# GeGLU on one core: raw rows of the first down projection fetched in front of stores, and the first pass's x transposed wholly on TensorE

## The chip, the cores and the metric

The kernel runs on one core of one Trainium2 chip. The metric is the device time of one execution in microseconds. A profile is one execution with every instruction recorded; its span is 1.7 to 2.2 us shorter than the device time of the same execution, for every kernel here.

Names used below: PE is TensorE, DVE is VectorE, ACT is ScalarE, POOL is GpSimd, SP is the engine that issues nearly all DMAs ("SPq" is its queue of instructions). `Lnnn` is a line of the kernel; many operations go through a helper and share its line. The granted clock is PE's clock as a share of full speed; PE is called cold while it is below 1. The DMA share is the mean busy share of the core's 16 DMA engines; transfers are counted in the window in which they start, so a short window can show a little over 1.

## The reference, cut to what matters

```python
B, S, Dm, Df = 1, 2048, 1024, 3584        # all bf16
def reference(x, w_gate, w_up, w_down):
    g = jnp.einsum("bsd,df->bsf", x, w_gate)
    u = jnp.einsum("bsd,df->bsf", x, w_up)
    h = _gelu(g) * u
    return jnp.einsum("bsf,fd->bsd", h, w_down)
```

## The kernel before

Rows of x are worked on in two passes of 1024 rows, each pass as two tiles of 512 rows (`xT[0]`, `xT[1]`, held transposed). A pass has 14 units, each of which makes 256 columns of `g` and `u` and from them a piece of `h`, and then a down projection. Both halves use a scheme with seven instead of eight block products, whose factors are sums of blocks: the `t` and `s` tiles in the units, the `m`/`made`, `td` and `q` tiles in the down projection. The sums of `w_down` are made once, in the first pass, stored to DRAM (`td`), and loaded from there by both passes. The two weight sums made last, of blocks 12 and 13, live in large buffers of the pool "w", which has three; the down projection's 1 MB loads of `td` use the same three buffers.

The down projection advances in steps. In steps 0 to 27 a step is four matmuls of 512 columns (0.86 us) that need raw rows of `w_down` (`rl`, fetched two blocks at a time by `fetch12`); from step 28 on it needs the sums (`q12`).

```python
    AT12 = [2, 2, 5, 5, 8, 8, 16, 18, 20, 22, 27, 29, 31, 33]   # step of each load12
    ...
    def store_made(j):
        nc.sync.dma_start(out=td[:, j], in_=made[j][:, :3].bitcast(f32))

    def load12(j):
        if j in BIG12:                                # BIG12 = (0, 2, 4): 1 MB each
            big = wpool.tile([P, 2, 2, N], f32, name="w")
            nc.sync.dma_start(out=big, in_=td[:, j : j + 2, :2])
    ...
    def fetch12(n):
        kh, j = n // 7, 2 * (n % 7)
        rl = slot([P, 2, N], bf16, "raw")
        nc.sync.dma_start(out=rl, in_=wdn[:, kh, j : j + 2, :N])
        raw[1, n] = rl
    ...
    for n in range(NJ):
        at(max(-1, 2 * n - 6), fetch12, n)            # needed from step 2 * n
    for j in range(NJ):
        at(AT12[j], load12, j)
    ...
            def prepare():                            # in every unit, first pass
                ...
                if js:                                # last unit: js = [11, 12, 13]
                    store_made(js[0])                 # waits for DVE's last sum of block 11
                for j in js[1:]:
                    keep_whole(j)                     # blocks 12, 13: sums on POOL
    ...
        def more(step):                               # runs after the fetches of its step
            if step in (-1, 1):
                store_made(NJ - 2 + (step > 0))       # blocks 12 and 13
            if step >= 16 and step % 2 == 0 and step // 2 - 8 < len(moves):
                c, ko = moves[step // 2 - 8]
                transposing(xT, c, ko, (2 * (ip + 1) + c) * N)    # next pass's x
```

The start: the first tile of x is loaded as rows (`xn`) and transposed on PE in pieces of 128x128 (`turn`), the second is transposed by eight DMAs. The weights of unit 1 come through ACT's queue.

```python
    xn0 = load_x(0)
    wf = wpool.tile([P, 2, NKB, 2 * P], bf16, name="w")
    for k0, k1 in ((0, 2), (2, 5), (5, NKB)):
        load_wf(nc.sync, k0, k1)
    for ko in range(NKB):
        transposing(xT, 1, ko, N)                     # dma_start_transpose
    ...
        for i in range(NS):
            turn(xT, xn0, 0, i, on_act if i == 1 else on_dve)
        w = load_w(1, nc.scalar, pinned=True)
        s = sums_s(w, dve)
        plain(bank[0:4], 0, range(0, 2), parts=2)     # unit 0, tile 0
        plain(bank[0:4], 0, range(2, NKB))
        ...
        plain(bank[4:8], 1, range(NKB))               # unit 0, tile 1
```

Of the kernel before, what the change touches and what calls it, by code (L numbers as in the profile page):

```python
# [10 lines left out]
def kernel(  # L11
# [23 lines left out]
    nc = tc.nc  # L35
    ENG = mybir.EngineType
    ORDER = {ENG.SP, ENG.DVE, ENG.Pool, ENG.PE}
    P = nc.NUM_PARTITIONS
# [12 lines left out]
    NKB = Dm // P  # L51
# [8 lines left out]
    SLOTS = 52  # L60
    LAG = 3
    BIG12 = (0, 2, 4)
    AT12 = [2, 2, 5, 5, 8, 8, 16, 18, 20, 22, 27, 29, 31, 33]
    AT12S = [2 * j + (j > 8) for j in range(NJ)]
    AT73 = [30 + 2 * j if j < 8 else 46 + j - 8 for j in range(NJ)]

# [9 lines left out]
    def new_x():  # L76
        return [xpool.tile([P, NKB, N], bf16, name=f"xT{c}") for c in range(2)]
# [36 lines left out]



    def load_w(u, queue=nc.sync, pinned=False):
        f0 = u * 2 * P
        w = wpool.tile([P, 2, NKB, 2 * P], bf16, name="w")
        for i, src in enumerate((w_gate, w_up)):  # L120
            got = queue.dma_start(
                out=w[:, i],
                in_=src[:, f0 : f0 + 2 * P].rearrange("(ko ki) f -> ki ko f", ki=P),
            )
            if queue is not nc.sync and not pinned:
                tc.keep_in_program_order(got)
        return w

# [7 lines left out]
    def sums_t(xT):  # L136
        K = range(KH)
        lo, hi = [[xT[c][:, k] for k in K] for c in range(2)], [
            [xT[c][:, KH + k] for k in K] for c in range(2)
        ]  # L140
        return Sums(
            how={
                "t1": lambda q: [new(dve, lo[1][k], lo[0][k], SUB, "t1") for k in K],
                "t2": lambda q: [new(dve, hi[1][k], q["t1"][k], SUB, "t2") for k in K],
                "t3": lambda q: [new(dve, hi[1][k], lo[1][k], SUB, "t3") for k in K],
                "t4": lambda q: [new(dve, hi[0][k], q["t2"][k], SUB, "t4") for k in K],
                "tb": lambda q: [cast(hi[1][k], "tb") for k in K],
            }
        )

    def sums_s(w, eng):
        GU = range(2)
        sh = [P, KH, P]
        a11, a21 = [[w[:, i, :KH, h : h + P] for i in GU] for h in (0, P)]
        a12, a22 = [[w[:, i, KH:, h : h + P] for i in GU] for h in (0, P)]
        return Sums(
            how={
                "s1": lambda q: [new(eng, a21[i], a22[i], ADD, "s1", sh) for i in GU],
                "s2": lambda q: [new(eng, q["s1"][i], a11[i], SUB, "s2", sh) for i in GU],
                "s3": lambda q: [new(eng, a11[i], a21[i], SUB, "s3", sh) for i in GU],  # L160
                "s4": lambda q: [new(eng, a12[i], q["s2"][i], SUB, "s4", sh) for i in GU],
                "sa": lambda q: [cast(a22[i], "sa", sh) for i in GU],
            }
        )
# [171 lines left out]
    def at(step, what, j):  # L336
        agenda.setdefault(int(step), []).append((what, j))

    for n in range(NJ):
        at(max(-1, 2 * n - 6), fetch12, n)  # L340
    for j in range(NJ):
        at(AT12[j], load12, j)
        at(AT12S[j], make12, j)
# [88 lines left out]
    def load_x(c):  # L432
        t = []
        for i in range(NS):
            xn = slot([P, Dm], bf16, "xn")
            r0 = c * N + i * P
            nc.sync.dma_start(out=xn, in_=x2[r0 : r0 + P, :])  # L437
            t.append(xn)
        return t
# [4 lines left out]
            nc.tensor.transpose(tp[:, ko, :], xn[i][:, ko * P : (ko + 1) * P], ident)  # L444
        copy(out=xT[c][:, :, i * P : (i + 1) * P], in_=tp)

    def transposing(xT, c, ko, r0):
        nc.sync.dma_start_transpose(  # L448
            out=xT[c][:, ko, :], in_=x2[r0 : r0 + N, ko * P : (ko + 1) * P]
        )  # L450

    def load_wf(queue, k0, k1):
        for i, src in enumerate((w_gate, w_up)):
            got = queue.dma_start(
                out=wf[:, i, k0:k1],
                in_=src[k0 * P : k1 * P, 0 : 2 * P].rearrange(
                    "(ko ki) f -> ki ko f", ki=P
                ),
            )
            if queue is not nc.sync:  # L460
                tc.keep_in_program_order(got)

    xT = new_x()
    xn0 = load_x(0)
    wf = wpool.tile([P, 2, NKB, 2 * P], bf16, name="w")
    for k0, k1 in ((0, 2), (2, 5), (5, NKB)):
        load_wf(nc.sync, k0, k1)
    for ko in range(NKB):
        transposing(xT, 1, ko, N)

    def plain(ps, c, kos, parts=1):
        n = N // parts
        for k in range(kos.start, kos.stop, 2):
            for part in range(parts):
                cols = slice(part * n, (part + 1) * n)
                for p, (j, i) in zip(ps, [(j, i) for j in range(2) for i in range(2)]):
                    for ko in (k, k + 1):
                        matmul(
                            p[:, cols],
                            wf[:, i, ko, j * P : (j + 1) * P],  # L480
                            xT[c][:, ko, cols],
                            ko == 0 and part == 0,
                            ko == NKB - 1,
                        )

    def finish(ps, c):
        for j in range(2):
            times(j, c, gelu(ps[2 * j]), ps[2 * j + 1])

    on_dve, on_act = nc.vector.tensor_copy, nc.scalar.copy  # L490
    t = sums_t(xT)
    with tc.manual_schedule(engines={ENG.Activation}):
        for _ in range(NWARM):
            nc.tensor.matmul(bank[3], lhsT=warm[:, :P], rhs=warm, start=True, stop=True)
        for i in range(NS):
            turn(xT, xn0, 0, i, on_act if i == 1 else on_dve)
        w = load_w(1, nc.scalar, pinned=True)
        s = sums_s(w, dve)
        plain(bank[0:4], 0, range(0, 2), parts=2)
        plain(bank[0:4], 0, range(2, NKB))  # L500
        t.make("t1")
        finish(bank[0:4], 0)
        s.make("s1", "s2")
        t.make("t2", "t3", "tb")
        s.make("s3", "sa")
        plain(bank[4:8], 1, range(NKB))
        finish(bank[4:8], 1)
# [8 lines left out]
    for ip in range(NPASS):  # L516
        for u in range(1 if ip == 0 else 0, NU):
            js = making(u) if ip == 0 else []

            def prepare():  # L520
                nonlocal ahead
                nxt["w"], nxt["s"] = ahead, None
                if u + 1 < NU:
                    nxt["s"] = make_s(ahead, pool)
                if u + 2 < NU:
                    ahead = load_w(u + 2)
                if js:
                    store_made(js[0])
                for j in js[1:]:
                    keep_whole(j)  # L530
                if ip == 0:
                    fetch_wd(making(u + 1))

            def keep(part, ps):
                if js:
                    keep_part(js[0], part, ps)

            def aside(part):
                nonlocal ahead
                if ahead is None:  # L540
                    ahead = load_w(2, nc.scalar)
                if part == 0 and "s4" not in s:
                    s.make("s4")
                    t.make("t4")

            def ahead_of_p4():
                if u + 1 < NU:
                    nxt["p1"] = first_product(even if u % 2 else odd, xT, nxt["w"])

            e = odd if u % 2 else even  # L550
            p1 = nxt.pop("p1", None) or first_product(e, xT, w)
            unit(u, (e, cc, dd), xT, w, s, t, p1, prepare, aside, keep, ahead_of_p4, ip == 0 and u == 1)
            if u + 1 < NU:
                w, s = nxt["w"], nxt["s"]

        last = ip == NPASS - 1
        got, nxt = {}, {}

        def more(step):

            nonlocal ahead
            if last:
                return
            if step in (-1, 1):
                store_made(NJ - 2 + (step > 0))
            if step == 0:
                xT[:] = new_x()
            if step >= 16 and step % 2 == 0 and step // 2 - 8 < len(moves):
                c, ko = moves[step // 2 - 8]
                transposing(xT, c, ko, (2 * (ip + 1) + c) * N)  # L570
            if step == 50:
                got["w"], ahead = load_w(0), load_w(1)
            if step == 58:
                got["s"] = make_s(got["w"], dve)
            if step == 62:
                got["t"] = make_t(xT)

        down(ip, even + cc, dd + odd, last, more)
        even, odd, cc, dd = odd, even, dd, cc
        if not last:  # L580
            w, t, s = got["w"], got["t"], got["s"]
# [29 lines left out]
```

## Time and profile before

| | before |
|---|---|
| time, median of the 3 runs at hand | 549.08 us (548.2 to 550.6) |
| span of the profile | 546.8 us |
| PE busy | 536.2 us, 98% |
| PE waits for raw rows of w_down, first pass | 4.6 us in 4 waits |
| PE waits for x at the start | 0.9 us (xT), 0.5 us (xn) |

PE is busy nearly all the time. These lines of the page are its busy time and the chain of work that ended last:

```profile
PE 536.2 (98%) x2405; PEld 378.7 (69%) x2405; DVE 341.3 (62%) x526; ACT 258.4 (47%) x463; POOL 236.2 (43%) x212
...
PE 92%; DMA 5%; SPq 2%; DVE 0%; issue 0%; ACT 0%; DVEq 0%; ACTq 0%
```

So only the gaps of PE can be won. The view of waits, for PE, has them all (total us, times, longest):

```profile
PE bank L111 <- DMA raw<-in_w_down_dram: 4.6, 4, 1.4
PE bank L494 <- DVE warm L428: 1.2, 1, 1.2
PE bank L111 <- DMA xT<-in_x_dram: 0.9, 2, 0.6
PE bank L444 <- DMA xn<-in_x_dram: 0.5, 1, 0.5
```

The view counts a gap from the modelled end of a matmul. Measured between starts, the four gaps for raw rows are 1.48, 1.52, 1.60 and 0.63 us, 5.2 us in sum. They lie at the head of the first down projection. The windows view of that stretch gives, for each window, its length, the busy time of PE, PEld, DVE, ACT and POOL, the granted clock, the DMA share and GB/s:

```profile
172.00:182.00 10.00, 10.00 (x47) 6.97 (x45) 6.33 (x11) 6.49 (x12) 5.95 (x6) 1.00 0.48 170
182.00:187.00 5.00, 4.42 (x20) 3.44 (x19) 4.09 (x7) 1.75 (x3) 1.04 (x1) 1.00 0.88 269
187.00:197.00 10.00, 8.79 (x40) 3.91 (x40) 9.76 (x16) 0.00 (x0) 0.00 (x0) 1.00 1.03 393
197.00:207.00 10.00, 7.22 (x32) 3.11 (x32) 8.94 (x14) 2.05 (x4) 0.00 (x0) 1.00 1.06 380
```

DMA is half idle before 182 and full after it. The timeline of SP's queue shows why (start, us, what it issued), and so does the first line of its waits from 180 to 216:

```profile
181.89 0.33 SPq L280 DMA_DIRECT2D td<-m  x1
182.31 2.62 SPq L329 DMA_DIRECT2D raw<-in_w_down_dram  x3
185.03 0.45 SPq L280 DMA_DIRECT2D td<-w  x1
185.53 0.42 SPq L329 DMA_DIRECT2D raw<-in_w_down_dram  x1
186.05 1.22 SPq L280 DMA_DIRECT2D td<-w  x1
187.36 1.55 SPq L329 DMA_DIRECT2D raw<-in_w_down_dram  x1
188.96 1.29 SPq L290 DMA_DIRECT2D w<-td  x1
190.30 1.26 SPq L329 DMA_DIRECT2D raw<-in_w_down_dram  x1
191.66 0.59 SPq L290 DMA_DIRECT2D w<-td  x1
```

```profile
SPq L280 <- DVE m L90: 8.6, 1, 8.6
```

SP issued nothing from 173.2 to 181.89, when DVE's sum for the store `td<-m` was made, and all raw fetches stand behind that store; from 180 to 182 the DMA share was 0.00. After it, every raw fetch stands behind a store of 768 KB or a load of 1 MB.

### The profile page before, as it was taken

Reading aid. Unit: us, or ns where it says so; the run is one execution under the profiler, and the core shown is the slowest. Engines: PE = TensorE matmul, PEld = TensorE weight load, DVE = VectorE, ACT = ScalarE, POOL = GpSimd, SP = SyncE. Lnnn points to the kernel's source line nnn. Section 1 sums busy time; section 2 is a strip of 40 time slices with the busy share of each in tenths; the row PEclk is TensorE's granted clock in tenths of the full one; section 3 lists DMA queues with packets and bytes.
Section 4 is the critical chain, followed back from the end, with each engine's and each line's share of the span. In section 5 each row is a group of like instructions: output and inputs, shape, how many; then the busy total and the mean of one; then the engine's idle time right before and its main releaser. Section 6 shows DMA issues by size and latency. Waiting matters only on the chain.

```text
span 546.8 us, 7414 instructions
## 1 busy us (share of the span) xinstructions
PE 536.2 (98%) x2405; PEld 378.7 (69%) x2405; DVE 341.3 (62%) x526; ACT 258.4 (47%) x463; POOL 236.2 (43%) x212
## 2 busy tenths in 40 slices
PE   8999999999999979999999999999999999999997
PEld 5477777667767635888877766776777775478885
DVE  3886766766666893585955555455555449766730
ACT  2466666566656410155445555555555551114431
POOL 0069966677774300000087777777777600000000
PEclk9999999999999999999999999999999999999999
DMA  8776666667645699999745222222222059373751
GB/s 210 168 199 174 173 180 203 197 179 208 199 146 173 229 383 289 308 197 276 263 134 135 78 79 77 78 77 79 77 78 77 0 199 381 133 230 97 226 187 49
DMA packets 108133, 93.28 MB, mean 171 GB/s; under 512 B 17216, under 2 KB 92992, under 8 KB 108096
## 3 DMA queue, kind: packets, MB, share of 16 engines
q1 hardware_dynamic: 103936, 90.72, 56.3%
q10 hardware_dynamic: 4160, 2.10, 1.5%
q8 instruction: 19, 0.31, 0.2%
q14 instruction: 18, 0.15, 0.1%
HBM read 74.45 MB, written 15.20 MB: 164 GB/s over the span
## 4 chain that ended last, share of the span: by engine, by line
PE 92%; DMA 5%; SPq 2%; DVE 0%; issue 0%; ACT 0%; DVEq 0%; ACTq 0%
PE bank L111 92%; DMA raw<-in_w_down_dram 3%; SPq L448 2%; DMA xT<-in_x_dram 1%; DMA xn<-in_x_dram 1%; DVE m L90 0%; SPq L437 0%; ACT bank L269 0%; ACT st L408 0%; SPq L280 0%; ACT u L107 0%; DVEq L90 0%; SPq L329 0%; ACTq L107 0%
## 5 line engine op out<-in xcount | busy, mean ns | idle before, releaser
L93 POOL TENSOR_TENSOR s<-w 128x512 fp32r<-128x512 bf16 x100 | 117.0, 1190 | 191.6 <-DVE t L90 92.8
L111 PE MATMUL bank<-t,s 128*128 128x512 f32 x648 | 157.0, 398 | 0.0
L111 PEld LDWEIGHTS bank<-t,s 128*128 128x128 f32 x648 | 121.8, 188 | 27.7
L111 PE MATMUL bank<-xT,w 128*128 128x512 bf16 (+1 forms) x504 | 116.5, 377 | 0.9 <-DMA xT<-in_x_dram 0.9
L107 ACT COPY p<-bank 128x512 f32<-128x512 f32 x124 | 70.4, 591 | 96.7 <-PE bank L111 96.7
L90 DVE TENSOR_TENSOR hT<-g,bank 128x512 bf16<-128x512 f32 x112 | 76.6, 687 | 54.7 <-ACT g L178 48.9
L111 PEld LDWEIGHTS <-w 128*128 128x128 bf16 x504 | 45.1, 98 | 60.3 <-issue 14.9
L90 DVE TENSOR_TENSOR sum<-bank,p 128x512 f32<-128x512 f32 x54 | 37.4, 692 | 53.2 <-PE bank L111 47.9
L178 ACT ACTIVATE g<-sum 128x512 f32<-128x512 f32 x81 | 51.5, 635 | 32.9 <-DVE sum L90 32.0
L111 PE MATMUL bank<-q 128*128 128x512 f32 x240 | 58.9, 389 | 0.0
L111 PE MATMUL bank<-t,sa 128*128 128x512 f32 x216 | 58.6, 413 | 0.0
L93 POOL TENSOR_TENSOR s<-w,s 128x512 fp32r<-128x512 bf16 x50 | 57.8, 1177 | 0.0
L93 POOL TENSOR_TENSOR s<-s,w 128x512 fp32r<-128x512 f32 x50 | 57.1, 1165 | 0.0
L111 PE MATMUL bank<-raw,hT 128*128 128x512 bf16 x224 | 49.2, 379 | 4.6 <-DMA raw<-in_w_down_dram 4.6
L111 PE MATMUL bank<-tb,s 128*128 128x512 f32 x216 | 53.3, 389 | 0.0
L111 PEld LDWEIGHTS bank<-q 128*128 128x128 f32 x240 | 45.1, 188 | 9.3
L111 PEld LDWEIGHTS bank<-t,sa 128*128 128x128 f32 x216 | 40.7, 188 | 10.6
L111 PEld LDWEIGHTS bank<-tb,s 128*128 128x128 f32 x216 | 40.6, 188 | 8.4
L102 ACT CAST tb<-raw 128x512 fp32r<-128x512 bf16 x28 | 17.2, 627 | 60.5 <-DMA raw<-in_w_down_dram 24.5
L107 ACT COPY u<-bank 128x512 f32<-128x512 f32 x62 | 35.9, 590 | 20.9 <-PE bank L111 19.2
L111 PEld LDWEIGHTS <-hT 128*128 128x128 bf16 x224 | 21.8, 98 | 31.6 <-issue 6.0
L90 DVE TENSOR_TENSOR bank<-bank,p 128x512 f32<-128x512 f32 x54 | 37.8, 700 | 8.2 <-PE bank L111 5.0
(44 smaller groups left out, 459.1 us busy)
## 6 DMA issues: line engine op xcount, KB each, us to landing
raw<-in_w_down_dram SPq DMA_DIRECT2D x80, 256.0 KB, 4.9
q<-td SPq DMA_DIRECT2D x60, 256.0 KB, 4.8
w<-in_w_gate_dram SPq DMA_DIRECT2D x25, 512.0 KB, 5.6
w<-in_w_up_dram SPq DMA_DIRECT2D x25, 512.0 KB, 6.5
td<-m SPq DMA_DIRECT2D x12, 768.0 KB, 4.6
w<-td SPq DMA_DIRECT2D x6, 1024.0 KB, 8.8
out_dram<-st SPq DMA_DIRECT2D x32, 128.0 KB, 1.7
td<-w SPq DMA_DIRECT2D x2, 768.0 KB, 6.7
```

The lines of the kernel that those rows point to most:

```text
L90: nc.vector.tensor_tensor(out=out, in0=a, in1=b, op=op)
L93: nc.gpsimd.tensor_tensor(out=out, in0=a, in1=b, op=op)
L102: nc.scalar.copy(out=t, in_=src)
L107: nc.scalar.copy(out=t, in_=ps)
L111: nc.tensor.matmul(ps, lhsT=lhs, rhs=rhs, start=start, stop=stop, skip_group_check=True)
L178: nc.scalar.activation(g, src, ACT.Gelu_apprx_tanh)
L448: nc.sync.dma_start_transpose(out=xT[c][:, ko, :], in_=x2[r0 : r0 + N, ko * P : (ko + 1) * P])
```

## The change: its intent, and the diff

The raw rows needed first are to be fetched before the stores, while DMA is idle, and everything not needed soon is to come later. At the start, DMA transposes are to be avoided: each takes 1.26 us of SP's time to issue, and PE waited for them. Cut to its core (the removal of helpers that are no longer needed is left out):

```diff
-    AT12 = [2, 2, 5, 5, 8, 8, 16, 18, 20, 22, 27, 29, 31, 33]
+    AT12 = [6, 6, 10, 10, 14, 14, 16, 18, 20, 22, 27, 29, 31, 33]
...
-        at(max(-1, 2 * n - 6), fetch12, n)
+        at(max(-1, 2 * n - 8), fetch12, n)
...
-    for ko in range(NKB):
-        transposing(xT, 1, ko, N)
+    xn1 = load_x(1)
+    w = load_w(1)                       # on SP instead of ACT's queue
...
-        plain(bank[0:4], 0, range(2, NKB))
+        plain(bank[0:4], 0, range(2, 4))
+        for i in range(2):
+            turn(xT, xn1, 1, i, on_act if i % 2 else on_dve)
+        plain(bank[0:4], 0, range(4, 6))
+        for i in range(2, NS):
+            turn(xT, xn1, 1, i, on_act if i % 2 else on_dve)
+        plain(bank[0:4], 0, range(6, NKB))
         (the sums t1, s1, t2, s2 are reordered a little around it)
...
-                if js:
+                if len(js) == 1:
                     store_made(js[0])
...
-            if step in (-1, 1):
-                store_made(NJ - 2 + (step > 0))
+            if step in (-1, 0, 2):
+                store_made({-1: NJ - 3, 0: NJ - 2, 2: NJ - 1}[step])
...
-            if step >= 16 and step % 2 == 0 and step // 2 - 8 < len(moves):
-                c, ko = moves[step // 2 - 8]
+            if step >= 24 and step % 2 == 0 and step // 2 - 12 < len(moves):
+                c, ko = moves[step // 2 - 12]
```

More of the change, by code (lines that the diff above doesn't have):

```diff
@@ L113, in matmul, with load_w @@
         )
-    def load_w(u, queue=nc.sync, pinned=False):
+    def load_w(u, queue=nc.sync):
         f0 = u * 2 * P
@@ L124, in load_w @@
             )
-            if queue is not nc.sync and not pinned:
+            if queue is not nc.sync:
                 tc.keep_in_program_order(got)
@@ L445, in turn @@
         copy(out=xT[c][:, :, i * P : (i + 1) * P], in_=tp)
-    def transposing(xT, c, ko, r0):
-        nc.sync.dma_start_transpose(
-            out=xT[c][:, ko, :], in_=x2[r0 : r0 + N, ko * P : (ko + 1) * P]
-        )
-    def load_wf(queue, k0, k1):
+    xT = new_x()
+    xn0 = load_x(0)
+    wf = wpool.tile([P, 2, NKB, 2 * P], bf16, name="w")
+    for k0, k1 in ((0, 2), (2, 5), (5, NKB)):
         for i, src in enumerate((w_gate, w_up)):
-            got = queue.dma_start(
+            nc.sync.dma_start(
                 out=wf[:, i, k0:k1],
@@ L459, in load_wf @@
             )
-            if queue is not nc.sync:
-                tc.keep_in_program_order(got)
-    xT = new_x()
-    xn0 = load_x(0)
-    wf = wpool.tile([P, 2, NKB, 2 * P], bf16, name="w")
-    for k0, k1 in ((0, 2), (2, 5), (5, NKB)):
-        load_wf(nc.sync, k0, k1)
-    for ko in range(NKB):
-        transposing(xT, 1, ko, N)
+    xn1 = load_x(1)
+    w = load_w(1)
     def plain(ps, c, kos, parts=1):
@@ L490 @@
     on_dve, on_act = nc.vector.tensor_copy, nc.scalar.copy
-    t = sums_t(xT)
+    s, t = sums_s(w, dve), sums_t(xT)
     with tc.manual_schedule(engines={ENG.Activation}):
@@ L496 @@
             turn(xT, xn0, 0, i, on_act if i == 1 else on_dve)
-        w = load_w(1, nc.scalar, pinned=True)
-        s = sums_s(w, dve)
         plain(bank[0:4], 0, range(0, 2), parts=2)
-        plain(bank[0:4], 0, range(2, NKB))
+        plain(bank[0:4], 0, range(2, 4))
[5 more added lines that the diff above has]
+        plain(bank[0:4], 0, range(6, NKB))
         t.make("t1")
+        s.make("s1")
         finish(bank[0:4], 0)
-        s.make("s1", "s2")
-        t.make("t2", "t3", "tb")
+        t.make("t2")
+        s.make("s2")
+        t.make("t3", "tb")
         s.make("s3", "sa")
@@ L563, in more @@
                 return
-            if step in (-1, 1):
-                store_made(NJ - 2 + (step > 0))
+            if step in (-1, 0, 2):
+                store_made({-1: NJ - 3, 0: NJ - 2, 2: NJ - 1}[step])
             if step == 0:
                 xT[:] = new_x()
-            if step >= 16 and step % 2 == 0 and step // 2 - 8 < len(moves):
-                c, ko = moves[step // 2 - 8]
-                transposing(xT, c, ko, (2 * (ip + 1) + c) * N)
+            if step >= 24 and step % 2 == 0 and step // 2 - 12 < len(moves):
+                c, ko = moves[step // 2 - 12]
+                r0 = (2 * (ip + 1) + c) * N
+                nc.sync.dma_start_transpose(
+                    out=xT[c][:, ko, :], in_=x2[r0 : r0 + N, ko * P : (ko + 1) * P]
+                )
             if step == 50:
```

## The prediction

> **What bounds it now.** TensorE: in the page's busy table PE has 98% of a 546.8 us span; the chain of waits is "PE bank" for 92%. Matmuls of 512 columns start 0.214 us apart nearly everywhere, so only PE's gaps can be won. Those that a DMA causes lie in two places (timeline; my gaps are start-to-start distances less the normal one, so a little over its "idle"):
>
> - Start: 0.50 us for xn (at 5.9), 0.50 and 0.74 us for the DMA-transposed xT (18.3 and 21.0).
> - Head of the first down projection: 1.48, 1.52, 1.60 and 0.63 us for raw rows of w_down (187.7, 197.9, 201.2, 205.3), 5.2 us in sum; the waits view says 4.6 us.
>
> The second pass, which stores nothing there, starts the same stage at 455.5 without a gap.
>
> **Why.** In the first pass the first three raw fetches stand in the queue behind a store that waits for DVE's last sum (181.9); the first lands 5.4 us later. DMA idles nearly from 175 to 182. From 182 to 216 it is full (windows view: share 0.9 to 1.12, 288 to 393 GB/s): three stores of 0.77 MB, three loads of 1 MB, raw rows, q loads and six transposes want the same 33 us. The Trainium skill ("DMA: Bandwidth & Descriptors", "Issuing engines are not separate DMA queues") says that all queues run on the same 16 engines and interleave; the saturation agrees, so order and bytes decide, not who issues.
>
> **Down head after.** Four fetches (1 MB, 3 us of DMA at 350 GB/s) go ahead of the stores into the idle time after 173; later ones come two steps (1.7 us) earlier; the 1 MB loads move from steps 2, 5, 8 to 6, 10, 14; six transposes (1.1 us of issue, 0.13 MB each) leave the stretch. In the second pass such fetches issue 15 us ahead, so buffers should be free. Estimate by bytes: 2.3 MB of stores, raw 4 to 9 and one or two big loads take 14 to 17 us after 182, done by 196 to 199; raw 9 is needed at 202. Nearly all of the 5.2 us goes; I leave 0.6.
>
> **Start after.** Added on PE: 32 transposes. Warm ones start 54 ns apart in the trace (105 ns cold): 1.8 us, all critical. (The skill, "TensorE: Matmul & The Clock Gate", "PE-mode transpose", has 275 to 390 ns for one; the pipelined 54 ns counts here.) Removed: 1.24 us of waits for xT, and 10.7 us of SP issue off the path. xn1 at about 330 GB/s lands between 9.5 and 12, where PE wants it at 10.8: up to 0.5 us of new wait. DVE gets two copies of 0.65 us, and its chain of sums ends near 28.6 while PE wants a bank at 28: 0.3 us more. Net +1.3 us.
>
> **Sum.** 549.1 - 4.6 + 1.3 = 545.8; predicted 545.6 us, 8 in 10 within 543.2 to 548.2. Faster by over 2%: 0.01; within 2%: 0.98; slower by over 2%: 0.01.
>
> **What would show it.** PE's waits for raw rows fall from 4.6 to under 1 us, the first fetch issued before 180; no PE wait for xT; unit 1's first product of sums starts 0.5 to 1.5 us after today's 25.8; the rest only shifts.
>
> **What would make it wrong.** Fetches held up by busy buffers or still by the queue's order; the delayed 1 MB loads as a new wait near 212; transposes until step 54 delaying the next stage's loads; DVE falling behind at 26 to 36 us.

## The result, and the profile after

The changed kernel took 543.73 us (median of 4 runs, 543.6 to 544.1); the kernel before, beside it on the same chip, 549.5 us (548.2 to 550.6, 4 runs). Executions over 1.5% slower than the fastest of the same kernel are left out of the means. Ratios here are the mean time of one kernel's runs over that of the other's runs of the same rounds, so not quite the ratio of the medians quoted: 0.9897, 95% interval 0.9873 to 0.992. That is 1.0% faster, clear of the noise but less than 2%. The prediction's range (543.2 to 548.2) holds it, 1.9 us below its centre.

The page's busy line, of the profile after, whose span is 542.0 us:

```profile
PE 537.1 (99%) x2437; PEld 379.6 (70%) x2437; DVE 342.9 (63%) x528; ACT 259.9 (48%) x465; POOL 237.0 (44%) x212
```

The 32 transposes are there (2437 matmuls instead of 2405). The view of waits for PE is now two lines:

```profile
PE bank L484 <- DVE warm L428: 1.2, 1, 1.2
PE bank L111 <- DMA w<-in_w_up_dram: 0.2, 1, 0.2
```

All waits for raw rows and for xT are gone; a small new one, for the weights of unit 2, has come in this profile (the view shows it in no other run). The same windows as before:

```profile
172.00:182.00 10.00, 10.00 (x46) 6.79 (x45) 6.46 (x11) 6.02 (x12) 4.37 (x4) 1.00 0.87 289
182.00:187.00 5.00, 5.00 (x24) 3.93 (x23) 4.40 (x7) 2.21 (x4) 2.63 (x3) 1.00 0.75 250
187.00:197.00 10.00, 10.00 (x48) 4.51 (x46) 9.66 (x16) 0.00 (x0) 0.00 (x0) 1.00 1.04 390
197.00:207.00 10.00, 10.00 (x48) 4.52 (x47) 9.18 (x15) 2.05 (x4) 0.00 (x0) 1.00 1.05 384
```

PE is busy throughout, the DMA share from 172 to 182 has risen from 0.48 to 0.87, and from 187 to 207 DMA is as full as it was. The timeline of SP's queue:

```profile
173.83 3.79 SPq L329 DMA_DIRECT2D raw<-in_w_down_dram  x4
182.49 0.34 SPq L280 DMA_DIRECT2D td<-m  x1
182.93 0.37 SPq L329 DMA_DIRECT2D raw<-in_w_down_dram  x1
183.40 0.91 SPq L280 DMA_DIRECT2D td<-w  x1
184.40 0.46 SPq L329 DMA_DIRECT2D raw<-in_w_down_dram  x1
184.95 1.54 SPq L280 DMA_DIRECT2D td<-w  x1
186.59 2.52 SPq L329 DMA_DIRECT2D raw<-in_w_down_dram  x2
189.16 1.02 SPq L290 DMA_DIRECT2D w<-td  x1
```

Four fetches are issued from 173.83, and eight before the first load of 1 MB, where it was five.

Where the time went, by the starts of the same matmuls in the two profiles:

| start of | before | after | difference, and what it adds |
|---|---|---|---|
| first product with sums in unit 1 | 25.76 | 26.02 | +0.26: the new start |
| first product with sums in unit 2 | 38.38 | 38.98 | +0.60: and 0.3 from the wait for unit 2's weights |
| first matmul with raw rows | 187.73 | 186.86 | -0.87: the first gap, 1.48, is gone |
| first matmul with sums of the down projection | 215.45 | 210.86 | -4.59: the other gaps, 3.7, are gone |
| first matmul with raw rows, second pass | 455.52 | 450.90 | -4.62 |
| end of the span | 546.8 | 542.0 | -4.8 |

From the first raw-row matmul to the first with sums is 24.0 us when nothing waits (112 matmuls). It was 27.72 before. "Gaps at the head" below is this stretch less 24.0 plus the gap just before it: 5.2 us before, 0 after.

### The profile page after: what moved, and what is told of

It is laid out like the page before. It is cut to its first block, busy times and chain, and to the rows that moved or that the text cites. A ratio compares the mean times of both kernels' runs of the same rounds, so it can differ in the third digit from the quotient of the medians.

```text
span 542.0 us, 7488 instructions
## 1 busy us (share of the span) xinstructions
PE 537.1 (99%) x2437; PEld 379.6 (70%) x2437; DVE 342.9 (63%) x528; ACT 259.9 (48%) x465; POOL 237.0 (44%) x212
## 4 chain that ended last, share of the span: by engine, by line
PE 96%; DMA 3%; SPq 1%; ACT 0%; issue 0%
PE bank L111 95%; DMA w<-in_w_up_dram 2%; DMA xn<-in_x_dram 1%; SPq L452 1%; SPq L437 0%; PE bank L444 0%; ACT st L408 0%; ACT p L107 0%
## 5 line engine op out<-in xcount | busy, mean ns | idle before, releaser
L90 DVE TENSOR_TENSOR q<-hT 128x512 fp32r<-128x512 bf16 x56 | 38.4, 687 | 5.1 <-PE bank L111 5.1
```

Of the source, the lines that this page charges most:

```text
L90: nc.vector.tensor_tensor(out=out, in0=a, in1=b, op=op)
```

## The experiments

All kernels gave correct results. Each was run with five rounds, and the kernel before ran 11 times beside each group of four; the three groups ran on three chips. Times are medians with ranges.

| run | time, us | before beside it, us | ratio (95%) | gaps at the head, us |
|---|---|---|---|---|
| down_only | 543.58 (542.91 to 544.0) | 548.09 | 0.991 (0.9893 to 0.9926) | 0 |
| start_only | 549.30 (548.93 to 550.06) | 548.09 | 1.0018 (1.0002 to 1.0035) | 5.1 |
| order_only | 545.42 (544.77 to 546.21) | 548.09 | 0.9942 (0.9924 to 0.9961) | 2.6 |
| room_only | 546.96 (546.02 to 548.23) | 548.09 | 0.9975 (0.9957 to 0.9994) | 2.7 |
| undo_tr | 543.73 (543.42 to 544.57) | 548.22 | 0.9922 (0.9909 to 0.9935) | 0 |
| undo_lead | 544.75 (544.35 to 545.43) | 548.22 | 0.9938 (0.9926 to 0.995) | 1.0 |
| turn_twice | 545.30 (545.17 to 546.11) | 548.22 | 0.9949 (0.9937 to 0.9961) | 0 |
| half_turn | 549.92 (549.16 to 550.79) | 548.22 | 1.0032 (1.0019 to 1.0046) | 0 |
| half_late | 542.87 (542.39 to 543.15) | 548.21 | 0.9892 (0.9871 to 0.9914) | 0 |
| undo_at | 545.44 (545.08 to 547.46) | 548.21 | 0.9945 (0.9923 to 0.9967) | 2.0 |
| undo_store | 546.06 (545.46 to 546.76) | 548.21 | 0.9954 (0.9932 to 0.9976) | 2.1 |
| after_again (the change) | 544.10 (543.60 to 545.65) | 548.21 | 0.9919 (0.9898 to 0.9941) | 0 |

### The base: after_again

The whole change, unedited, on the chip of the last group.

> The whole change again on the same chip as the three others, as their base. Expected 0.991 of before, within 0.002, no wait for raw rows.

It came out at 544.10 us and 0.9919, with no wait for raw rows.

### Which half of the change: down_only and start_only

`down_only` is the kernel before with every edit of the down projection (the edits of `AT12`, `fetch12`, `store_made` and the step of the transposes, as in the diff above) and the old start. `start_only` is the whole change with those five edits put back.

> The kernel before with all of the change at the down projection (fetches four ahead, stores behind them, big loads later, next-pass transposes from step 24) and the old start. Theory: the gain comes from the down head alone, all four gaps close, about 5.2 us below before, and since the new start costs 0.3 to 0.6 us this is 0.3 to 0.6 us faster than the whole change. Rival: the new start is worth time too, then this lies 0.5 us or more above the whole change.

> The whole change with everything at the down projection put back; only the start is new. Theory: 32 transposes of 54 ns (1.75 us) less 1.24 us of removed waits, and about 0.3 us for a later w load: 0.3 to 0.9 us slower than before. Rival: DMA transposes taken off the queue pay for more than the PE's ones, 0.5 us or more faster than before.

The down projection brings the whole gain: 4.5 us between the medians of down_only and before, with no wait for raw rows left. The new start costs time: start_only is 1.2 us above before by the medians, 1.0 us by the ratio (0.1 to 1.9 us; about 0.3 us of it lies outside the span, which was 2.1 to 2.2 us shorter than the time in every run of start_only and 1.8 to 1.9 us in those of before beside it), and its gaps at the head are all there (5.1 us). down_only was expected 0.3 to 0.6 us faster than the whole change; the ratios to before (0.991 and 0.9919, on two chips) agree with 0.5 us, but their intervals overlap, so this comparison alone does not show it.

### Order in the queue or bytes: order_only and room_only

```diff
 order_only, against before: only these
-        at(max(-1, 2 * n - 6), fetch12, n)
+        at(max(-1, 2 * n - 8), fetch12, n)
-                if js:
+                if len(js) == 1:
-            if step in (-1, 1): ...
+            if step in (-1, 0, 2): ...
 room_only, against before: only these
-    AT12 = [2, 2, 5, 5, 8, 8, 16, ...
+    AT12 = [6, 6, 10, 10, 14, 14, 16, ...
-            if step >= 16 and ...            (transposes of the next pass)
+            if step >= 24 and ...
```

> Before with the queue order alone: raw fetches four ahead and in front of the three stores; big loads stay at steps 2, 5, 8 and transposes at 16. Theory A (queue order: the raw rows stood behind a store that waits for sums while DMA was idle): at least 4 of the 5.2 us of gaps go. Rival B (bytes: too much wanted between 182 and 216): only the first gap, 1.5 us, goes, and the later three stay at over 2.5 us in sum.

> Before with only the big loads moved to steps 6, 10, 14 and the transposes to step 24; fetches and stores in the old order. Theory A (queue order): the first gap of 1.5 us stays and at least 3.5 us of gaps in sum. Rival B (bytes): the first gap stays, the three later ones, 3.7 us, go.

Neither edit is enough alone. order_only closed 2.6 of the 5.2 us, room_only 2.5, and the two together all of it: in the profiles the parts add up. Theory A's numbers failed in both runs. Rival B's came out in order_only (2.6 us of later gaps, over the 2.5 forecast) and failed in room_only, where the later gaps fell from 3.7 to 1.1 us and not to nothing. In time room_only gained only 1.1 us between medians (1.4 us by the ratio, 0.3 to 2.4), less than its one profile says; this was not explained. The waits of PE for raw rows, first in order_only, then in room_only:

```profile
PE bank L111 <- DMA raw<-in_w_down_dram: 1.9, 2, 1.4
```

```profile
PE bank L111 <- DMA raw<-in_w_down_dram: 2.1, 4, 1.4
```

What is left in room_only is the first gap (1.59 us, as expected) and three small late ones of 0.36 to 0.39 us, which were not expected. For what is left in order_only, the timeline of SP's queue suggested a cause:

```profile
185.28 1.41 SPq L290 DMA_DIRECT2D w<-td  x1
186.74 1.08 SPq L280 DMA_DIRECT2D td<-w  x1
187.91 0.39 SPq L329 DMA_DIRECT2D raw<-in_w_down_dram  x1
189.93 0.36 SPq L290 DMA_DIRECT2D w<-td  x1
190.38 1.31 SPq L329 DMA_DIRECT2D raw<-in_w_down_dram  x2
196.38 0.37 SPq L290 DMA_DIRECT2D w<-td  x1
196.84 2.38 SPq L329 DMA_DIRECT2D raw<-in_w_down_dram  x4
```

SP stands from 191.7 to 196.38 in front of the third load of 1 MB. The waits of SP's queue from 180 to 216 say for what:

```profile
SPq L290 <- DMA td<-w: 6.2, 2, 4.7
```

The load needs the buffer of block 13's sums, which comes free when their store has landed. The queue is served in order, so four raw fetches stand behind it. The trace's landing times agree to 0.02 us: the stores landed at 189.91 and 196.37, the loads were issued at 189.93 and 196.38. This gave a third theory, C: the blocked head of the queue makes these raw rows late.

The trace does not bear C out. The windows view of order_only over a stretch that holds most of this wait:

```profile
186.00:195.00 9.00, 8.95 (x42) 4.10 (x42) 8.36 (x13) 0.38 (x1) 0.00 (x0) 1.00 1.02 360
```

DMA was full while SP stood (from 191.7 to 196.38 the share was 1.02, at 406 GB/s): what had been issued before went on landing until 201.08. The third load landed 2.68 us after that; in the kernel before, where SP did not stand there, it landed 2.57 us after the same raw rows. And the largest gap left, 1.56 us at 200.40, belongs to raw rows that were issued at 190.38, before the wait; they landed at 200.35, 0.68 us after the 1 MB load in front of them (SP had stood 1.5 us before that load too, with a DMA share of 1.01 from 187 to 191). The first rows issued after the wait landed at 204.52, 0.76 us after the third load, and cost 0.70 us. So what the trace shows is the place in line: raw rows behind a load of 1 MB, with DMA full. A run without the wait but with the same order was not made.

The later gaps of the kernel before look the same: raw rows land behind the 1 MB load issued in front of them, and PE starts with them at that moment. Landing times are taken from the trace's semaphores:

```
before: raw rows    issued   landed   1 MB load in front landed   PE starts with them
  5                 190.30   197.84   197.11                      197.88
  6                 192.35   201.16   200.41                      201.20
  8                 194.54   205.24   204.47                      205.28
```

### Which of the two moves made the room: undo_at and undo_tr

`undo_at` is the whole change with `AT12` as before; `undo_tr` is the whole change with the transposes of the next pass from step 16 as before.

> The whole change, but the next pass's transposes back at step 16. In order_only the three 1 MB loads stand in the queue until a store has landed (4.7 us for the third) and the raw fetches stand behind them. Theory C (blocked queue head): the moved loads alone cure the later gaps, the first transpose is issued only near 202, so nothing comes back: raw-row waits under 0.3 us, time within 0.5 us of the whole change. Rival B (bytes): six transposes back in the stretch bring back 1 us or more of raw-row waits.

> The whole change with the 1 MB loads back at steps 2, 5 and 8. Theory C (blocked queue head): the queue stands still for several us before the second and third of these loads, until a store has landed, and the raw fetches behind it come late: 1.5 to 2.5 us of raw-row gaps, as in order_only. Rival: order_only's gaps came from its transposes, then there is none here.

undo_tr has no wait for raw rows at all, and 543.73 us: putting the transposes back brings nothing back. undo_at brings back 2.0 us of gaps, 1.3 us in time against after_again on the same chip. The waits of SP's queue in undo_at, same window, have the standing queue that theory C expected:

```profile
SPq L290 <- DMA td<-w: 6.1, 2, 4.2
```

So the moved 1 MB loads did all of the room's work, and rival B, as far as it blamed the transposes, falls. C's number came out (1.5 to 2.5 us of gaps were expected), but its mechanism is not shown: in undo_at too DMA was full while SP stood (share 1.03 from 191.58 to 195.79), and its two gaps, 1.37 and 0.66 us, end with raw rows that landed 0.74 and 0.75 us after a load of 1 MB. What undo_at shows is that the place of these loads in the line matters.

### What the order did: undo_store and undo_lead

```diff
 undo_store, against the whole change
-                if len(js) == 1:
+                if js:
-            if step in (-1, 0, 2): ...
+            if step in (-1, 1): ...           (as before)
 undo_lead, against the whole change
-        at(max(-1, 2 * n - 8), fetch12, n)
+        at(max(-1, 2 * n - 6), fetch12, n)
```

> The whole change with the store of the third-last sum back in the last unit, in front of all fetches (the lead of eight steps and the late big loads stay). Expected: the first fetch is issued after 182 as before, the first gap of 1.3 to 1.6 us is back, and 0 to 1 us of later gaps, since the idle time before 182 is lost: 1.3 to 2.5 us slower than the whole change.

> The whole change with the fetches six steps ahead again instead of eight; stores stay behind the first fetches (three instead of four in front). If the lead itself matters, 0.5 us or more of raw-row waits come back; if getting in front of the store is all, none does and the time is that of the whole change within 0.5 us.

undo_store is 2.0 us slower than after_again. Its first gap is 0.82 us, smaller than expected (the first raw rows landed at 187.32 instead of 187.69 before, and PE, behind the slower start, came for them 0.3 us later), and 1.27 us come later, a little more than expected: the four fetches that would have used the idle time before 182 now stand among everything else. undo_lead is 1.0 us slower than undo_tr on the same chip, with gaps of 0.61 and 0.39 us that end at 208.2 and 210.4, at the end of the raw rows. So getting in front of the store is not all: the lead is worth a microsecond too. Whether it was the one fetch fewer before 182, or all later fetches standing two steps further back, was not told apart.

### The price of the transposes: turn_twice

```diff
+        for ko in range(NKB if c == 1 else 0):
+            nc.tensor.transpose(tp[:, ko, :], xn[i][:, ko * P : (ko + 1) * P], ident)
         copy(out=xT[c][:, :, i * P : (i + 1) * P], in_=tp)
```

> The whole change with each of the 32 new transposes done twice (same result). If a transpose costs its warm start-to-start distance of 54 ns on the critical path: 1.7 us slower than the whole change. If they hide in waits for xn or sums: under 0.7 us. If a mode change or a colder clock costs more: over 2.5 us.

Against undo_tr, which has the same start, ran on the same chip and also has no gap at the head, 32 more transposes cost 1.57 us, 49 ns each. That is near the distance at which warm transposes start in the traces, 56 ns (107 ns cold; the prediction's 54 and 105 were read a little low), as far as two medians whose runs spread over about 1 us can say: they are on the critical path.

### An attempt to beat both: half_turn and half_late

```diff
 half_turn, against the whole change
-    xn1 = load_x(1)
+    xn1 = load_x(1, KH * P)                  # only the first 512 columns of these rows
     w = load_w(1)
+    for ko in range(KH, NKB):
+        nc.sync.dma_start_transpose(
+            out=xT[1][:, ko, :], in_=x2[N : 2 * N, ko * P : (ko + 1) * P]
+        )
+    ahead2 = load_w(2)                       # half_late: without this line ...
 (turn transposes and copies only ko < 4 for the second tile)
-    ahead = None
+    ahead = ahead2                           # ... and without this one
```

> An attempt to beat both: the whole change, but of x's second tile only the first four of eight column blocks go through TensorE (16 transposes), the other four by DMA behind the first w load, and the second w load issued in the idle time after that. Expected: 0.9 us for 16 transposes and 0.3 us for the w load saved, so 1.2 us below the whole change, with no wait for xT. If the DMA transposes land later than their use, a wait for xT shows and eats it.

> half_turn with the second w load back at its old, late place (queued by ScalarE in unit 1). In half_turn PE waited 4.5 us for DVE: with w there early, GpSimd's sums ran beside DVE's (two GpSimd sums took 7.0 us, four DVE sums 6.3 us instead of 2.5). If that collision is all, the 4.5 us wait is gone, DVE's four t4 sums take 2.5 us again, and the 16 saved transposes leave it 0.5 to 0.9 us below the whole change. Rival: half the transposes on DMA delay the sums anyway, then the wait stays.

half_turn failed: 549.92 us, though its first product with sums of unit 1 starts at 25.56, earlier than in any kernel with 32 new transposes. Its waits of PE:

```profile
PE bank L111 <- DVE sum L90: 4.5, 1, 4.5
```

The timeline of DVE, and then of POOL, in half_turn:

```profile
28.91 3.08 DVE L90 TENSOR_TENSOR s<-w,s 128x512 fp32r<-128x512 bf16 x2
31.92 6.33 DVE L90 TENSOR_TENSOR t<-xT,t 128x512 fp32r<-128x512 bf16 x4
```

```profile
21.76 6.99 POOL L93 TENSOR_TENSOR s<-w 128x512 fp32r<-128x512 bf16 x2 [20.46 <-DMA w<-in_w_gate_dram]
28.71 2.74 POOL L93 TENSOR_TENSOR s<-s,w 128x512 fp32r<-128x512 f32 x2
31.41 3.17 POOL L93 TENSOR_TENSOR s<-w 128x512 fp32r<-128x512 bf16 x2
```

With the weights of unit 2 there early, POOL began its sums at 21.76, in the middle of DVE's, and the two got into each other's way: first POOL's sums took 3.5 us each while DVE kept its pace, then DVE's slowed down. In half_late, whose only difference is the late load of these weights, POOL starts at 31.52 and the same DVE sums take less than half as long:

```profile
28.91 1.28 DVE L90 TENSOR_TENSOR s<-w,s 128x512 fp32r<-128x512 bf16 x2
30.11 2.49 DVE L90 TENSOR_TENSOR t<-xT,t 128x512 fp32r<-128x512 bf16 x4
```

The Trainium skill ("GPSIMD Engine Reference", "1. Specifications") says that GpSimd's interfaces to SBUF are shared with VectorE and contended by its instructions with two SBUF inputs. These runs agree: DVE's sums of two SBUF tiles went from 0.62 to 1.58 us each (6.33 against 2.49 for four), while DVE's sums with a PSUM operand kept their 0.68 us beside POOL's work.

The wait of 4.5 us then cost a second time. The windows view of half_turn, just after it:

```profile
40.00:46.00 6.00, 6.00 (x17) 3.24 (x17) 4.02 (x7) 2.41 (x6) 6.00 (x6) 0.55 0.01 1
```

The granted clock is 0.55, and twelve matmuls start 0.427 instead of 0.216 us apart, some 2.6 us. The Trainium skill ("TensorE: Matmul & The Clock Gate", "Part 1: The HAM clock gate") says that the clock halves after an idle window of about 3.4 us and that 512 columns then take 426.7 ns; this agrees. The gaps of 1.5 us at the head of the down projection were too short for it: the clock there was 1.00 in the windows view.

half_late is 542.87 us against 544.10 for after_again on the same chip; the ranges do not touch (542.39 to 543.15, 543.60 to 545.65). It is 1.2 us below the change and 5.3 us below the kernel before. Its first product with sums of unit 1 starts at 25.56.

## Why the prediction was right or wrong

- **PE bounds, only its gaps count: right.** The gain is gaps closed; but for the start and the 0.2 us at the end (see Sum), the rest only shifted.
- **The first gap comes from fetches behind a store that waits for DVE: right.** Freed, they were issued at 173.83, before 180 as predicted, and undo_store brings a first gap and 2.0 us back.
- **The later gaps come from a full queue, so order and bytes decide: right in the main, wrong in a part.** Raw rows 4 to 9 had landed by 197.87, within the 196 to 199 of the estimate by bytes. Neither part is enough alone: fetches in front and the old place of the loads leave 2.6 us (order_only), moved loads and the old fetches 2.7 us (room_only). But the step "six transposes ... leave the stretch" earned nothing (undo_tr).
- **"Nearly all of the 5.2 us goes; I leave 0.6": the term was 0.6 us too small.** All of it went.
- **Start, "Net +1.3 us": too large.** Seven profiles with the new start and 32 transposes have the first product with sums of unit 1 at 26.02 to 27.14, mean 26.41; four with the old one at 25.76 to 26.12, mean 25.97. That is 0.44 us, and 0.50 us at unit 2; timing says 1.0 us (0.1 to 1.9). The added 1.8 us is about right (1.57 us measured by doubling). Two terms were mis-sized. The "up to 0.5 us of new wait" for xn1 varies from profile to profile: 0.22 us in that of the change, 1.0 us in undo_tr. The old start is worth less than its one profile said: in down_only and order_only the view has 0.8 and 1.1 us of wait for the first rows of x instead of 0.5, none for xT, and PE was cold until 10.1 and 9.7 us instead of 7.1, so that removing the wait for xT would not have earned the same there. "0.3 us more" for DVE at 28 us did not show. The wait for unit 2's weights, 0.3 us, which the prediction did not have, came in the change's own profile and in none of the other six. Why timing gives more than the profiles is open.
- **Sum.** Predicted was 3.5 us below the 549.08 us at hand. The profiles give 4.8 us of span: 5.2 less 0.6, and 0.2 at the tail. The tail comes with the new start: from the first raw-row matmul of the second pass to the end of the span it is 91.0 to 91.1 us in the eight kernels with all of x's second tile on PE, and 91.3 us in the six others, though PE's last matmul starts at the same 87.45 us in all fourteen. The first timing gave 5.8 us between medians, but after_again, beside 11 runs of before, gave 4.1 us (544.10 against 548.21). In these three later groups before had medians of 548.09, 548.22 and 548.21, so about 1 us of the first timing is before's own scatter (547.5 to 551.3 in one group).

What stays open: why the tail after the last matmul is 0.2 us shorter with the new start, whether the queue standing before a load costs anything by itself, and how much of undo_lead's loss is the one fetch in the idle time and how much the two steps.

## What to carry to other kernels

A DMA queue that is served in order must be read as a list: a store that waits for a sum holds back every small urgent fetch behind it while DMA idles, and once DMA is full, each bulk load in front of an urgent fetch delays it by its bytes (in the kernel before, the second and third load of 1 MB landed 2.57 us after the transfer in front of them). So put urgent fetches first and bulk loads as late as their use allows. A wait at the queue's head is not yet a cause: look whether DMA ran dry during it (here it did for the store that waited for a sum, and not for the loads that waited for a buffer). When two edits look like one cure, run each alone and each undone: here two halves added up, and a third edit did nothing. Loading something earlier into idle DMA time is no gift if it lets another engine start beside the critical one; the same early load cost 7 us here.

## What the Trainium skill lacked or had wrong

- "TensorE: Matmul & The Clock Gate", "PE-mode transpose": it gives 275 to 390 ns for a 128x128 bf16 transpose. In a row, these start 56 ns apart on a warm PE (107 ns cold), and 32 more cost 1.57 us, 49 ns each; this kernel is priced by that distance. The section gives no such distance for transposes; the page's start-to-start times, in its Part 1, are for matmuls.
- "GPSIMD Engine Reference", "1. Specifications": it names the contention with VectorE instructions of two SBUF inputs but no size there (nor does "SBUF — State Buffer", which tells more of the shared ports, give durations of such sums). Here such VectorE sums went from 0.62 to 1.58 us each, and two GpSimd sums took 6.99 us where POOL's mean for that group is 1.19 us each.
- "DMA: Bandwidth & Descriptors", "Two DMAs through the same engine are not ordered": it asks that the issuing engine wait for the first DMA's semaphore, and does not say there what that wait does to later DMAs of the queue. Here one such wait held SP for 4.7 us with four fetches behind it, while DMA stayed full (share 1.02) from what had been issued before.
- The same page, "Issuing engines are not separate DMA queues", on which the prediction leans: nothing here contradicts it, but no run tested it, for none issued the raw rows from a second engine.
